# Four slots of a fused attention and gated-MLP kernel get a hand-written order of work on every engine

## The chip, the cores and the metric

The kernel runs on one core of one Trainium2 chip. A core has five engines that run side by side, each from its own queue: TensorE (PE in the profile; the loading of its weights is PEld), VectorE (DVE), ScalarE (ACT), GpSimd (POOL) and SyncE (SP), whose queue issues nearly all DMAs. The metric is the device time of one execution in microseconds, the median of several runs. Before the change it is 759.58 us (three runs, 759.41 to 760.52).

## The reference

```python
def _attn_ref(q, k, v):                      # 8 batches, 8 heads, 576 rows, 64 columns
    scores = scale * np.matmul(q, k.transpose(0, 1, 3, 2))
    scores = np.where(mask, scores, -1e9)    # causal in blocks of 64
    scores = scores - np.max(scores, axis=-1, keepdims=True)
    attn = np.exp(scores)
    attn = attn / (np.sum(attn, axis=-1, keepdims=True) + 1e-09)
    return np.matmul(attn, v)

def _moe_ref(x, w_in, g_ln, w_sg, b_sg, w_out):   # x: 8 x 576 x 512, all heads side by side
    h = gelu_tanh(x @ w_in)                  # 1024 columns
    u, v = h[..., :512], h[..., 512:]
    v_n = (v - mu) / np.sqrt(var + 1e-06) * g_ln  # LayerNorm over columns
    v_s = einsum('ts,bsd->btd', w_sg, v_n) + b_sg[None, :, None]
    return x + (u * v_s) @ w_out
```

The weights w_in, w_out and others arrive as float64 words; results are float32.

## The kernel before

**Accuracy by splits.** TensorE multiplies in float32r, which keeps fewer bits than float32. So every operand x is held as two tiles, hi (x cast to float32r) and lo (x − hi), and each product is made of three: hi·hi, lo·hi, hi·lo. The splits are work for the other engines: q and k on POOL (`split_qk`, line 116, four instructions per slot), the weights on POOL (`split_weight`, line 190, a cast and a subtraction), the attention output x (xh on VectorE, xl on POOL).

**Slots.** The outer loop (line 840) runs over 32 pairs of heads, four to a batch; one round of it is a slot. In slot n TensorE turns (transposes) the probabilities of pair n: pA, pB, pC, then pd and pe, which hold the diagonal blocks and the inverse row sums; the copies ptA, ptB, ptC and rb bring them from PSUM to SBUF (`turn`, `turn_sums`). It makes the scores s of pair n + 1 in two halves (`first` and `second`, each two steps), and between the halves the values product ob of pair n. VectorE takes the maxima and writes prob and negm from the scores, ScalarE makes the exponentials and their sums, VectorE normalises ob to x, and x is written to DRAM (spill) and split.

**FF pieces in the holes.** The MLP of a batch (`feed_forward`, line 542) is cut into pieces that stand in a queue, `work`, and `hole(k)` issues the next k of them between the parts of attention: five v pieces (accv), eight u pieces (accu), eight s pieces (accs, the spatial product) and eight o pieces (acco). A digit string such as "1112" gives the pieces of a slot's four holes. Side steps hang beside them in the queue `side` (line 517): the gelu of v, then five `moments` (bn_stats and bn_aggr), `inverse_std` (rs, on POOL), five `centre` and five `scale` steps (vh on ScalarE, vl on VectorE, the last tile's vn_t and vone on VectorE). `run_side(k)` runs the next k. An s piece needs all of them, and the split spatial weights ws_h and ws_l.

**Weights.** They are loaded and split once, during the first eight slots and a little after. A part is 128 x 256 float64 values. Its sign, exponent and mantissa words are put together to float32 by ScalarE (the Abs of the high word), and three VectorE instructions on words (one shift, two merges), tiles w; POOL then splits it. `load_weight` and `load_spatial` are generators, and each `next` issues one step. v's columns come first, then u's, then the spatial weights (four tiles ws_h/ws_l of 128 rows, then the ends, with the bias b_sg in a zero-filled tile), then w_out.

**Who sets the order.** Slots 0 to 3 (`opening_slot`) hold no FF pieces; there every engine runs in the order in which the program is written (`written`, lines 50 and 145). From slot 4 on only TensorE does (line 842); for the others the framework's scheduler picks the order with a timeline of its own, and weights are issued by `load_share` at places that the table WS gives. PSUM has eight banks (`bank`, line 81), each held from its first product to its last reader. SBUF pages come from small pools: five buffers "pt", shared by the copies ptA to ptC, two buffers "xr" for spatial weights, w_out parts and reloaded spills, two "x", and one each for q_f, k_f and their splits.

Every helper goes through one method (line 60), so the profile gives L60 for almost all instructions and the tiles' names tell them apart.

Of the kernel before, what the change touches and what calls it, by code (L numbers as in the profile page):

```python
# [20 lines left out]
def kernel(  # L21
# [169 lines left out]
        gpsimd.tensor_copy(dh, x)  # L191
        gpsimd.tensor_tensor(dl, x, dh.bitcast(F32), op=ALU.subtract)

    class Double:


        def __init__(self, raw, name):
            n = raw.shape[-1]
            words = raw.bitcast(U32).rearrange("p (n t) -> p n t", t=2)
            self.hi, self.lo = words[:, :, 1], words[:, :, 0]  # L200
            tm = page(U32, 2 * n, name)
            self.t, self.m = tm[:, :n], tm[:, n:]
            scalar.activation(
                self.m.bitcast(F32), self.hi.bitcast(F32), AF.Abs, scale=2.0**-112
            )

        def single(self, words=None):
            t = self.t
            x = t if words is None else words
            vector.tensor_scalar(x, self.lo, 29, None, op0=ALU.logical_shift_right)  # L210
            vector.scalar_tensor_tensor(
                x, self.hi, 0x80000000, x, op0=ALU.bitwise_and, op1=ALU.bitwise_or
            )
            vector.scalar_tensor_tensor(
                t, self.m, 3, x, op0=ALU.logical_shift_left, op1=ALU.bitwise_or
            )
            return t.bitcast(F32)

    def load_weight(part, src, cols, dh, dl, name="w", ahead=2, groups=()):

        W = 256
        parts = [(c, slice(f, f + W)) for f in range(cols.start, cols.stop, W) for c in range(NC)]
        raws = {}

        def fetch(k):
            if k < len(parts):
                c, fs = parts[k]
                raws[k] = page(src.dtype, W, name)
                sync.dma_start(raws[k], src[c * P : (c + 1) * P, fs])

        for k in range(ahead):
            fetch(k)
        if part == "v":
            yield False
        k = 0
        for size in (*groups, *([1] * len(parts))):
            if k == len(parts):
                return
            opened = []
            for j in range(k, k + size):  # L240
                fetch(j + ahead)
                raw = raws.pop(j)
                opened.append(raw if src.dtype == F32 else Double(raw, name))
            yield False
            if src.dtype != F32:
                words = []
                for j, x in enumerate(opened):
                    if part == "v" and j % 2 == 0:
                        t = bank("w").bitcast(U32)
                        words += [t[:, :W], t[:, W:]]  # L250
                opened = [x.single(*words[j : j + 1]) for j, x in enumerate(opened)]
            yield False
            for j, x in zip(range(k, k + size), opened):
                c, fs = parts[j]
                split_weight(x, dh[:, c, fs], dl[:, c, fs])
            k += size
            yield True

    def load_spatial():
        t = page(F32, S, "x")  # L260
        gpsimd.memset(t[BLK:, :DH], 1.0)
        vector.tensor_copy(vone[BLK:, :], t[BLK:, :DH])

        def fetch(j):
            t = page(F32, S, "xr")
            if j < NT - 1:
                sync.dma_start(t, w_sgT[j * P : (j + 1) * P, :])
            elif j == NT - 1:
                for hf in (0, 1):
                    sync.dma_start(t[hf * BLK : (hf + 1) * BLK, :], w_sgT[j * P : S, :])  # L270
            else:
                gpsimd.memset(t[BLK:, :], 0.0)
                sync.dma_start(t[BLK : BLK + 1, :], b_sg.unsqueeze(0))
                sync.dma_start(t[96:97, :], b_sg.unsqueeze(0))
            return t

        raws = deque(fetch(j) for j in (0, 1))
        sync.dma_start(g_bc, g_ln.unsqueeze(0).broadcast_to([P, DH]))
        yield True
        for j in range(NT - 1):  # L280
            split_weight(raws.popleft(), ws_h[:, j, :], ws_l[:, j, :])
            raws.append(fetch(j + 2))
            yield True

        j = NT - 1
        t, t2 = raws
# [8 lines left out]
        yield True  # L295

    weights = deque(
        [
            ("v", load_weight("v", w_in, slice(DH, DFF), wi_h, wi_l, "w", 3, (3, 2, 2, 1))),
            ("u", load_weight("u", w_in, slice(0, DH), wi_h, wi_l)),  # L300
            ("s", load_spatial()),
            ("o", load_weight("o", w_out, slice(0, DM), wo_h, wo_l, "xr", 0)),
        ]
    )

    def weight_half():

# [121 lines left out]
    class Values:  # L429
# [21 lines left out]

# [253 lines left out]
    def hole(k=1):  # L705
# [17 lines left out]

# [16 lines left out]
    def opening_slot(n, va):  # L740
# [37 lines left out]

    def slot(n, va):
        nx = n + 1 < N  # L780
        k = 6 if n // Q == 1 else 3
        g = [int(x) for x in (FIRST if n // Q == 1 else PLAN)[n % Q]]
        if n + 1 < N:
            load_v(n + 1)
# [22 lines left out]
        if nx:  # L807
            nx.second()
        load_share(n, 2)
        if n == Q + 1:  # L810
            run_side(2 * NT + 1)
        if n % Q == Q - 1:
            va.split()
        else:
# [80 lines left out]
```

## Time and profile before

| | |
|---|---|
| median of the runs | 759.58 us |
| the profiled execution | 758.6 us |
| its span, first to last instruction | 756.8 us |
| TensorE busy | 735.5 us, 97% of the span |
| VectorE, ScalarE, GpSimd busy | 467.4, 427.4, 302.2 us |
| mean granted TensorE clock | 0.995 |

The profiled execution is one run, recorded by the hardware. Its span is 1.8 us shorter than its time. Rows of groups show busy time, mean ns of one instruction, and the idle time ahead of it with what ended it; `A <- B` in the waits says that A waited for B. In a timeline a row is start, duration, engine, operation and tiles, and in brackets the idle time ahead. Matmul ends are modelled, so a busy TensorE may still be held back a little.

### The profile page before, as it was taken

What the parts mean: (1) busy time and instruction counts of PE and PEld (TensorE: products, weight loads), DVE (VectorE), ACT (ScalarE), POOL (GpSimd) and SP (SyncE); (2) the same over time, 40 slices, a digit from 0 to 9 for tenths busy, and PEclk for the clock granted to TensorE, in tenths of its full rate; (3) what the DMA queues carried; (4) which work ended last, traced back from release to release, by engine and by line L of the source; (5) the groups of instructions that cost most, each with busy time, mean ns of one, the idle gap of its engine ahead of it and who ended that gap; (6) DMA issues with size and microseconds to landing.
All of it is one profiled execution on the core that took longest, in us unless ns stands there. A gap on an engine that the chain in (4) does not pass through costs nothing.

```text
span 756.8 us, 18453 instructions
## 1 busy us (share of the span) xinstructions
PE 735.5 (97%) x6942; PEld 691.2 (91%) x6942; DVE 467.4 (62%) x1473; ACT 427.4 (56%) x1068; POOL 302.2 (40%) x376
## 2 busy tenths in 40 slices
PE   8999878999999999999999999999999999999997
PEld 6887877989899899999999899998999989998997
DVE  5985869765855369544776348663495545941732
ACT  6894947457644678337764377544873467721500
POOL 3864865644445323243433234351234532322121
PEclk9999999999999999999999999999999999999999
DMA  6545432333342223322233122621234221220032
GB/s 177 169 129 173 127 102 72 98 95 97 110 151 71 65 77 95 106 67 71 71 118 118 33 70 78 187 56 49 66 91 148 71 60 51 61 83 16 6 122 94
DMA packets 84301, 70.05 MB, mean 93 GB/s; under 512 B 59891, under 2 KB 59891, under 8 KB 84213
## 3 DMA queue, kind: packets, MB, share of 16 engines
q1 hardware_dynamic: 84068, 68.58, 30.9%
q8 instruction: 55, 0.90, 0.5%
q10 hardware_dynamic: 144, 0.29, 0.1%
q14 instruction: 34, 0.27, 0.1%
HBM read 49.98 MB, written 18.87 MB: 91 GB/s over the span
## 4 chain that ended last, share of the span: by engine, by line
PE 80%; DVE 6%; ACT 5%; DMA 3%; POOL 2%; issue 2%; DVEq 0%; SPq 0%; ACTq 0%
PE accs L60 15%; PE acco L60 13%; PE accv L60 12%; PE accu L60 11%; PE s L60 10%; PE ob L60 9%; ACT prob L60 3%; PE pd L60 3%; PE pA L60 3%; PE pB L60 3%; DVE prob L60 2%; DMA xr<-in_w_out 2%; PE pC L60 2%; PE pe L60 1%; DVE w L60 1%
## 5 line engine op out<-in xcount | busy, mean ns | idle before, releaser
L60 ACT ACTIVATE prob<-prob,negm 128x576 f32<-128x576 f32 (+3 forms) x320 | 176.6, 555 | 68.0 <-DVE negm L60 66.9
L60 DVE CUSTOM_DVE_ANT_0 prob<-s,mask 128x256 f32<-128x256 f32 (+3 forms) x320 | 119.6, 418 | 42.8 <-PE s L60 41.4
L60 POOL TENSOR_TENSOR xh<-x,xh 128x64 fp32r<-128x64 f32 x32 | 10.5, 328 | 193.2 <-DVE xh L60 171.4
L60 POOL TENSOR_TENSOR gl<-u,gh 128x288 fp32r<-128x288 f32 x64 | 52.2, 820 | 87.1 <-DVE gh L60 71.6
L60 PE MATMUL accu<-xh,wi_h 128*128 128x288 f32 x256 | 78.7, 307 | 3.1 <-DVE negm L60 3.1
L60 PE MATMUL acco<-gh,wo_h 128*128 128x288 f32 x256 | 77.5, 303 | 1.7 <-ACT ptB L60 1.4
L60 PE MATMUL accs<-ws_h,vh 128*128 128x288 f32 x256 | 77.9, 304 | 0.0
L60 PE MATMUL accu<-xh,wi_l 128*128 128x288 f32 x256 | 76.0, 297 | 0.0
L60 PE MATMUL accu<-xl,wi_h 128*128 128x288 f32 x256 | 76.0, 297 | 0.0
L60 PE MATMUL accs<-ws_h,vl 128*128 128x288 f32 x256 | 75.5, 295 | 0.0
L60 PE MATMUL accs<-ws_l,vh 128*128 128x288 f32 x256 | 75.4, 295 | 0.0
L60 PE MATMUL acco<-gh,wo_l 128*128 128x288 f32 x256 | 75.4, 295 | 0.0
L60 PE MATMUL acco<-gl,wo_h 128*128 128x288 f32 x256 | 75.4, 294 | 0.0
L60 PE MATMUL accv<-wi_h,xh 128*128 128x512 f32 x160 | 65.3, 408 | 1.1 <-DVE negm L60 1.1
L60 PE MATMUL s<-kh,qh 64*128 64x320 f32 (+4 forms) x384 | 64.4, 323 | 2.0 <-ACT kh L60 1.3
L60 DVE TENSOR_TENSOR u<-accs,u 128x288 f32<-128x288 f32 x64 | 29.3, 457 | 56.6 <-PE accs L60 55.6
L60 PE MATMUL s<-kh,ql 64*128 64x320 f32 (+4 forms) x384 | 60.0, 303 | 3.9 <-POOL ql L60 3.9
L60 PE MATMUL accv<-wi_l,xh 128*128 128x512 f32 x160 | 62.8, 392 | 0.0
L60 ACT ACTIVATION_READ_ACCUMULATOR prob<-prob,negm 128x1 f32 x320 | 60.3, 189 | 0.0
L60 PE MATMUL s<-kl,qh 64*128 64x320 f32 (+4 forms) x384 | 58.8, 302 | 0.3 <-DVE kl L60 0.3
L60 ACT COPY vv<-accv 128x512 f32<-128x512 f32 x32 | 18.6, 581 | 64.8 <-PE accv L60 64.8
L60 PEld LDWEIGHTS accu<-xh,wi_h 128*128 128x128 f32 x256 | 48.5, 189 | 4.7 <-issue 3.0
(116 smaller groups left out, 2081.1 us busy)
## 6 DMA issues: line engine op xcount, KB each, us to landing
q_f<-in_qT SPq DMA_DIRECT2D x32, 288.0 KB, 3.4
spill<-x SPq DMA_DIRECT2D x32, 288.0 KB, 2.8
xr<-spill SPq DMA_DIRECT2D x32, 288.0 KB, 3.0
out_T<-xr SPq DMA_DIRECT2D x32, 288.0 KB, 3.1
k_f<-in_kT SPq DMA_DIRECT2D x31, 288.0 KB, 3.3
v_f<-in_v SPq DMA_DIRECT2D x32, 128.0 KB, 2.9
v_d<-in_v SPq DMA_DIRECT2D x64, 64.0 KB, 2.6
v_f<-in_v SPq DMA_DIRECT2D x64, 64.0 KB, 2.6
```

What stands on the lines that cost most here:

```text
L60: return lambda *a, **k: pin(method(*a, **k), self.letter)
```

## The change

The float64 weights are handled in pairs of parts (size 2): two Abs, two shifts and two merges of 256 columns into a PSUM bank, one merge of 512 columns, and one cast and one subtraction of 2 x 256 on POOL in place of two each. w_out keeps single parts, now in the "pt" buffers. The DMAs of all weights stand in one list, `coming`, and `fetch(k)` issues the next k where the script says. Slots 4 to 7 become `middle_slot`, and every engine runs them in the order written; six entries of SCRIPT a slot say what is issued between the parts of attention. Slots from 8 on stay with the scheduler. In slots 4 to 7 the ptC copy goes to ScalarE. On TensorE nothing moves: its rows are the same, but for 10 filler transposes in place of 16 ahead of slot 0.

```diff
-    class Double:
-            scalar.activation(
-                self.m.bitcast(F32), self.hi.bitcast(F32), AF.Abs, scale=2.0**-112
-            )
...
+    def fetch(k=1):
+
+        for _ in range(k):
+            coming.popleft()()
...
+    def load_weight(src, off, cols, dh, dl, name, size):
...
+            raw = [raws.popleft() for _ in range(size)]
...
+            if size == 2:
+                m = page(U32, size * W, name)
+            else:
+                tm = sp.tile([P, 2 * W], U32, tag="pt", name="tm", bufs=5)
+                t, m = tm[:, :W], tm[:, W:]
+            for j, x in enumerate(words):
+                scalar.activation(
+                    m[:, j * W : (j + 1) * W].bitcast(F32),
+                    x[:, :, 1].bitcast(F32),
+                    AF.Abs,
+                    scale=2.0**-112,
+                )
+            yield False
+            if size == 2:
+                t = page(U32, size * W, name)
+                y = bank("w").bitcast(U32)
+            else:
+                y = t
+            for j, x in enumerate(words):
+                yj = y[:, j * W : (j + 1) * W]
+                vector.tensor_scalar(yj, x[:, :, 0], 29, None, op0=ALU.logical_shift_right)
+                vector.scalar_tensor_tensor(
+                    yj, x[:, :, 1], 0x80000000, yj, op0=ALU.bitwise_and, op1=ALU.bitwise_or
+                )
+            vector.scalar_tensor_tensor(
+                t, m, 3, y, op0=ALU.logical_shift_left, op1=ALU.bitwise_or
             )
...
+            split_weight(t, *dst)
             yield True
...
+    def fetch_ends():
+        t = page(F32, S, "xr")
+        for hf in (0, 1):
+            sync.dma_start(t[hf * BLK : (hf + 1) * BLK, :], w_sgT[(NT - 1) * P : S, :])
+        t2 = page(F32, S, "xr")
+        gpsimd.memset(t2[BLK:, :], 0.0)
+        sync.dma_start(t2[BLK : BLK + 1, :], b_sg.unsqueeze(0))
+        sync.dma_start(t2[96:97, :], b_sg.unsqueeze(0))
+        raws.extend((t, t2))
...
-            copy("a" if which == "C" and self.n < Q else TE[which], pt, t)
+            copy("a" if which == "C" and self.n < 2 * Q else TE[which], pt, t)
...
-    WS = {
-        4: (0, 4, 0, 2),
...
+    WS = {8: (0, 0, 1, 3), 9: (0, 0, 0, 2)}
...
+        fetch(2 if n < Q - 1 else 4)
...
+    def weigh(k=1):
+        for _ in range(k):
+            weight_half()
+
+    SCRIPT = {
+        4: (
+            lambda: (fetch(2), weigh(1)),
+            lambda: weigh(3),
+            lambda: (fetch(2), weigh(3)),
+            lambda: None,
+            lambda: weigh(3),
+            lambda: (fetch(3), weigh(2)),
+        ),
+        5: (
+            lambda: (run_gelu(), weigh(1), fetch(1)),
+            lambda: run_side(2),
+            lambda: (run_side(3), weigh(1), fetch(1)),
+            lambda: run_side(1),
+            lambda: weigh(1),
+            lambda: None,
+        ),
+        6: (
+            lambda: (run_side(5), weigh(1), fetch(1)),
+            lambda: (run_side(4), weigh(1)),
+            lambda: run_side(1),
+            lambda: None,
+            lambda: fetch(1),
+            split_pending,
+        ),
+        7: (
+            lambda: None,
+            lambda: None,
+            lambda: None,
+            lambda: weigh(2),
+            lambda: weigh(1),
+            lambda: weigh(3),
+        ),
+    }
+
+    def middle_slot(n, va):
...
+        va.turn("A0")
+        va.turn("A1")
+        if n != 2 * Q - 2:
+            split_pending()
+        hole(g[0])
+        script[0]()
+        va.turn("B0")
+        va.turn("B1")
+        hole(g[1])
+        script[1]()
+        va.turn("C")
+        va.turn_sums()
+        hole(g[2])
+        script[2]()
+        nx = Scores(n + 1)
+        nx.first()
+        va.products()
+        va.normalise()
+        nx.second()
...
+        nv.inverse()
+        script[3]()
+        split_qk(n + 2)
+        script[4]()
+        hole(g[3])
+        script[5]()
+        return nx, nv
...
-    warm(bank("warm"), 16)
+    warm(bank("warm"), 10)
...
-        if n == Q:
+        if n == 2 * Q:
             written.intersection_update("P")
-        sc, va = (opening_slot if n < Q else slot)(n, va)
+        sc, va = (opening_slot, middle_slot, slot)[min(n // Q, 2)](n, va)
```

What moves is best seen on three engines. First VectorE in the first half of slot 4, before (ISA with prob and negm is the maximum step on the scores s, and w are the words of u's columns):

```order
L60 COPY ptA_1076<-pA_1075 128x512
L60 TENSOR_SCALAR r<-sums 128x10
L60 RECIPROCAL r<-r 128x10
L60 COPY ptB_1105<-pB_1104 128x512
L60 COPY ptC<-pC 128x512
L60 TENSOR_SCALAR w<-w 128x256
L60 SCALAR_TENSOR_TENSOR w<-w 128x256
L60 TENSOR_SCALAR w<-w 128x256
L60 SCALAR_TENSOR_TENSOR w<-w 128x256 x2
L60 TENSOR_SCALAR w<-w 128x256
L60 ISA prob_110,negm<-s,mask 128x256
L60 ISA negm 128x1
```

and after:

```order
L60 COPY ptA_1065<-pA_1064 128x512
L60 COPY ptB_1101<-pB_1100 128x512
L60 TENSOR_SCALAR w<-w 128x256
L60 SCALAR_TENSOR_TENSOR w<-w 128x256
L60 TENSOR_SCALAR w<-w 128x256
L60 SCALAR_TENSOR_TENSOR w<-w 128x256
L60 SCALAR_TENSOR_TENSOR w<-w 128x512
L60 TENSOR_SCALAR w<-w 128x256
L60 SCALAR_TENSOR_TENSOR w<-w 128x256
L60 TENSOR_SCALAR w<-w 128x256
L60 SCALAR_TENSOR_TENSOR w<-w 128x256
L60 SCALAR_TENSOR_TENSOR w<-w 128x512
```

The words of one part, and the last steps of others among the maxima, have become the words of two groups of two parts, all ahead of the first maximum.

Second, POOL around slot 6, before (ws_h and ws_l are the split spatial weights, rs LayerNorm's inverse deviation, sums and xr fills, qh to kl the splits of the pair after next):

```order
L60 TENSOR_TENSOR ws_l<-xr,ws_h 128x576 x2
L60 CAST kh<-k_f 128x576
L60 CAST qh<-q_f 128x576
L60 MEMSET sums 128x2
L60 CAST ws_h<-xr 128x576 x2
L60 TENSOR_TENSOR kl<-k_f,kh 128x576
L60 TENSOR_SCALAR rs<-stats 128x5
L60 TENSOR_TENSOR ql<-q_f,qh 128x576
L60 TENSOR_TENSOR ws_l<-xr,ws_h 128x576 x2
L60 TENSOR_TENSOR rs<-rs,half 128x5
L60 MEMSET xr 64x576
L60 CAST ws_h<-xr 128x576
```

and after:

```order
L60 TENSOR_SCALAR rs<-stats 128x5
L60 TENSOR_TENSOR rs<-rs,half 128x5
L60 CAST qh<-q_f 128x576
L60 TENSOR_TENSOR ql<-q_f,qh 128x576
L60 CAST kh<-k_f 128x576
L60 TENSOR_TENSOR kl<-k_f,kh 128x576
L60 CAST ws_h<-xr 128x576
L60 TENSOR_TENSOR ws_l<-xr,ws_h 128x576
L60 CAST ws_h<-xr 128x576
L60 TENSOR_TENSOR ws_l<-xr,ws_h 128x576
L60 MEMSET xr 64x576
L60 CAST ws_h<-xr 128x576
```

The four steps of q and k stood among the spatial weights and rs; now rs, then q and k whole, then each spatial tile with its cast and subtraction together.

Third, ScalarE in slot 6, before (u copies a u piece from PSUM, vh is LayerNorm's scale step, the cast ws_l the row of the bias):

```order
L60 COPY ptB_1745<-pB_1744 128x512
L60 COPY u<-accu 128x288
L60 COPY rb<-pd 128x512
L60 COPY rb<-pe 128x384
L60 COPY u<-accu 128x288
L60 ACTIVATE prob_107,sums<-prob_107,negm 128x192 x2
L60 ACTIVATE vh<-vv,rs 128x512 x3
L60 CAST ws_l<-xr 64x576
```

and after:

```order
L60 COPY ptB_1694<-pB_1693 128x512
L60 COPY u<-accu 128x288
L60 ACTIVATE vh<-vv,rs 128x512 x3
L60 CAST ws_l<-xr 64x576
L60 COPY ptC<-pC 128x512
L60 COPY rb<-pd 128x512
L60 COPY rb<-pe 128x384
L60 COPY u<-accu 128x288
L60 ACTIVATE vh<-vv,rs 128x512
```

The scale steps and the bias cast stood behind the rb copies, among the exponentials; now three of them and the bias cast stand ahead of ptC and rb.

More of the change, by code (lines that the diff above doesn't have):

```diff
@@ L192, in split_weight @@
         gpsimd.tensor_tensor(dl, x, dh.bitcast(F32), op=ALU.subtract)
-    class Double:
[L197 to L202, printed above, removed]
-            scalar.activation(
-                self.m.bitcast(F32), self.hi.bitcast(F32), AF.Abs, scale=2.0**-112
-            )
[L207 to L212, printed above, removed]
-            )
[L214 to L233, printed above, removed]
-            yield False
[L235 to L256, printed above, removed]
@@ new lines, with fetch_weight, fetches @@
+    W = 256
+    raws = deque()
+    coming = deque()
+    def fetch(k=1):
+        for _ in range(k):
+            coming.popleft()()
+    def fetch_weight(src, c, fs, name):
+        t = page(src.dtype, W, name)
+        sync.dma_start(t, src[c * P : (c + 1) * P, fs])
+        raws.append(t)
+    def fetches(src, cols, name):
+        for f in range(cols.start, cols.stop, W):
+            for c in range(NC):
+                coming.append(lambda c=c, f=f: fetch_weight(src, c, slice(f, f + W), name))
@@ L262, in load_spatial @@
         vector.tensor_copy(vone[BLK:, :], t[BLK:, :DH])
[L264 to L279, printed above, removed]
         for j in range(NT - 1):
             split_weight(raws.popleft(), ws_h[:, j, :], ws_l[:, j, :])
-            raws.append(fetch(j + 2))
             yield True
         j = NT - 1
-        t, t2 = raws
+        t, t2 = raws.popleft(), raws.popleft()
         gpsimd.tensor_copy(ws_h[:, j, :], t)
@@ L295, in load_spatial, with fetch_spatial, fetch_gain @@
         yield True
+    def fetch_spatial(j):
+        t = page(F32, S, "xr")
+        sync.dma_start(t, w_sgT[j * P : (j + 1) * P, :])
+        raws.append(t)
+    def fetch_ends():
+        t = page(F32, S, "xr")
+        for hf in (0, 1):
[5 more added lines that the diff above has]
+        raws.extend((t, t2))
+    def fetch_gain():
+        sync.dma_start(g_bc, g_ln.unsqueeze(0).broadcast_to([P, DH]))
     weights = deque(
         [
-            ("v", load_weight("v", w_in, slice(DH, DFF), wi_h, wi_l, "w", 3, (3, 2, 2, 1))),
-            ("u", load_weight("u", w_in, slice(0, DH), wi_h, wi_l)),
+            ("v", load_weight(w_in, DH, DH, wi_h, wi_l, "w", 2)),
+            ("u", load_weight(w_in, 0, DH, wi_h, wi_l, "w", 2)),
             ("s", load_spatial()),
-            ("o", load_weight("o", w_out, slice(0, DM), wo_h, wo_l, "xr", 0)),
+            ("o", load_weight(w_out, 0, DM, wo_h, wo_l, "xr", 1)),
         ]
     )
+    fetches(w_in, slice(DH, DFF), "w")
+    fetches(w_in, slice(0, DH), "w")
+    coming.append(fetch_gain)
+    for j in range(NT - 1):
+        coming.append(lambda j=j: fetch_spatial(j))
+    coming.append(fetch_ends)
+    fetches(w_out, slice(0, DM), "xr")
     def weight_half():
@@ L780, in slot @@
         nx = n + 1 < N
-        k = 6 if n // Q == 1 else 3
+        k = 3
         g = [int(x) for x in (FIRST if n // Q == 1 else PLAN)[n % Q]]
@@ L826, in slot @@
         return nx, nv
+    def weigh(k=1):
[36 more added lines that the diff above has]
+    def middle_slot(n, va):
+        script = SCRIPT[n]
+        g = [int(x) for x in FIRST[n % Q]]
+        load_v(n + 1)
+        load_qk(n + 2)
+        va.turn("A0")
[17 more added lines that the diff above has]
+        nx.second()
+        if n % Q == Q - 1:
+            va.split()
+        else:
+            pending.append(va.split)
+        nv = Values(n + 1, nx)
+        nv.inverse()
[5 more added lines that the diff above has]
+        return nx, nv
     pending = []
@@ L832 @@
     load_qk(1)
-    next(weights[0][1])
+    fetch(2)
     sc = Scores(0)
```

28 lines of the change are left out of this document (21 added, 7 removed).

## The prediction

> **What bounds the kernel now.** I read the page's first part, then a table of windows cut at the first pA transpose of each slot (slot n treats head pair n; slot 4 starts at 53.0 us), then TensorE's waits, then the timelines where TensorE stood still.
>
> ```profile
> span 756.8 us, 18453 instructions
> PE 735.5 (97%) x6942; PEld 691.2 (91%) x6942; DVE 467.4 (62%) x1473; ACT 427.4 (56%) x1068; POOL 302.2 (40%) x376
> ...
> 53.00:76.80 23.80, 22.62 (x184) 19.14 (x183) 14.92 (x52) 12.85 (x36) 11.76 (x17) 1.00 0.55 159
> 76.80:95.10 18.30, 16.00 (x175) 15.01 (x174) 15.54 (x48) 17.22 (x44) 15.69 (x21) 1.00 0.42 129
> 95.10:120.30 25.20, 18.52 (x176) 17.74 (x175) 19.22 (x43) 11.94 (x31) 15.79 (x14) 0.89 0.29 79
> 120.30:145.90 25.60, 24.94 (x239) 23.85 (x238) 22.32 (x64) 17.22 (x43) 15.90 (x20) 0.98 0.31 92
> 145.90:168.00 22.10, 22.10 (x184) 18.99 (x183) 13.52 (x44) 10.23 (x28) 10.08 (x15) 1.00 0.34 101
> 168.00:191.20 23.20, 22.38 (x224) 21.53 (x223) 12.72 (x46) 18.71 (x48) 11.41 (x17) 1.00 0.34 98
> 191.20:215.00 23.80, 22.26 (x225) 21.46 (x224) 21.12 (x61) 16.96 (x39) 10.85 (x11) 1.00 0.37 116
> ...
> 239.10:261.10 22.00, 22.00 (x183) 18.95 (x182) 8.98 (x34) 10.88 (x29) 6.35 (x9) 1.00 0.20 55
> 261.10:283.10 22.00, 22.00 (x224) 21.48 (x223) 11.52 (x40) 16.63 (x41) 6.48 (x9) 1.00 0.29 78
> 283.10:305.00 21.90, 21.90 (x224) 21.39 (x223) 18.91 (x55) 16.50 (x36) 9.19 (x10) 1.00 0.36 113
> 305.00:329.10 24.10, 24.10 (x240) 23.59 (x239) 14.11 (x47) 8.70 (x25) 10.16 (x14) 1.00 0.33 95
> ```
>
> The columns are the stretch, its length, busy time of PE, PEld, DVE, ACT and POOL, the granted clock, and the DMA share. TensorE is busy for 735.5 of 756.8 us: it is the bound. The last four rows are slots 12 to 15, with TensorE never idle at full clock; they show what a slot costs when nothing makes it wait. Slot 12 holds five v pieces (22.0), slot 13 eight u pieces (22.0), slot 14 eight o pieces (21.9), slot 15 eight s pieces (24.1). Slots 4, 8, 9, 10 and 7 hold the same TensorE work as 12, 12, 13, 14 and 15. Slots 5 and 6 hold four u pieces; one piece is
>
> ```profile
> 86.17 1.59 PE accu L60 x12
> ...
> 89.34 2.80 PE ob L60 x56
> ...
> 92.26 1.25 PE s L60 x12
> ```
>
> (chain of waits) 1.59 us, so their floor is 22.0 − 4 × 1.59 = 15.6. What each slot loses against its floor: slot 4, 23.8 − 22.0 = 1.8; slot 5, 18.3 − 15.6 = 2.7; slot 6, 25.2 − 15.6 = 9.6; slot 7, 25.6 − 24.1 = 1.5; slot 8, 0.1; slot 9, 23.2 − 22.0 = 1.2; slot 10, 23.8 − 21.9 = 1.9. Together 18.8 us. The order on TensorE is the same row for row before and after, but for six filler transposes; so the change can only give back waits, and these 18.8 us are nearly all there is.
>
> ```profile
> PE s L60 <- POOL ql L60: 3.9, 1, 3.9
> PE accu L60 <- DVE negm L60: 3.1, 2, 2.8
> PE accv L60 <- DVE negm L60: 1.1, 1, 1.1
> ...
> 103.28 0.38 PE L60 MATMUL s<-kh,qh 64*128 64x256 f32 x2
> 107.53 0.43 PE L60 MATMUL s<-kh,ql 64*128 64x256 f32 x2 [3.86 <-POOL ql L60]
> ```
>
> Slot 6 is the large one: TensorE's score products stand 3.9 us for the split of q on POOL, then 2.8 us for VectorE. The clock falls after each: 0.89 of 25.2 us and 0.98 of 25.6 us leave out 2.8 + 0.5 = 3.3 us, 1.65 us for each of the two waits.
>
> **The change, slot by slot.** All times below are from the slot's first pA.
>
> Opening slots: VectorE's word work goes from 3, 2, 2, 1 weight parts to 2 each, the same eight parts. Slot 0 is relieved of one part, slot 3 gets one more. By
>
> ```profile
> L60 DVE SCALAR_TENSOR_TENSOR w<-w 128x256 uint32<-128x256 uint32 x32 | 14.5, 466 | 1.3
> L60 DVE TENSOR_SCALAR w<-w 128x256 uint32<-128x256 uint32 x16 | 7.8, 499 | 4.7 <-DMA w<-in_w_in 4.6
> ```
>
> a part is 0.50 + 2 × 0.47 = 1.4 us, so the bounds are −1.0 and +0.9; I take 0. The six filler transposes fewer ahead of slot 0 lie under ScalarE's first exponentials:
>
> ```profile
> 10.09 4.01 ACT prob L60 x15
> ...
> 56.91 0.87 PE pB L60 x8
> ```
>
> that chain of waits runs through them, not through the fillers: 0, and at most 6 × 0.87 / 8 = 0.65 if it did not.
>
> Slot 4. The words of the first u columns were fetched here and came late:
>
> ```profile
> 64.75 0.39 PE L60 MATMUL s<-kh,qh 64*128 64x256 f32 x2
> ...
> 65.20 0.29 DVE L60 TENSOR_SCALAR w<-w 128x256 uint32<-128x256 uint32 x1 [3.50 <-DMA w<-in_w_in]
> ...
> 68.51 0.41 DVE L60 CUSTOM_DVE_ANT_0 prob<-s,mask 128x256 f32<-128x256 f32 x1
> ```
>
> VectorE stood 3.5 us for the DMA, then did words while the scores, begun at 64.75, waited until 68.51; their banks came free late and the next v piece stood 1.1 us. Afterwards the first four parts are fetched in slot 3, and two groups of two parts stand ahead of the scores on VectorE: four shifts, four 256-wide merges and two 512-wide ones (between 0.47 and 0.94, I take 0.7) are 5.3 us, from the ptB copy at about 5.4 to 10.7, while scores come at 64.75 − 53.0 = 11.7. They fit with 1 us over. Left: 0.4 (0 to 1.8), for the extra part in slot 3.
>
> Slot 5. After the reciprocal (1.5 before the slot) VectorE does two more groups (5.3) and the vv add, then ptA, the xh cast and the 1.0-fill copy to vone, then ptB, and five
>
> ```profile
> L580 DVE BATCH_NORM_STATS2 bs<-vv 128x6 f32<-128x512 f32 x8 | 5.3, 661 | 0.0
> ```
>
> with their aggregates, some 4 us, ahead of the softmax of the scores. I reach 11 us there; the scores are ready at 8.7. A new wait stands in that row: vone reads a tile that POOL fills only behind the last w split and xl. TensorE has ob (2.8) to do meanwhile and six banks in use, so only the second half of the next scores and one u piece feel it. Left: 0.8 (0 to 2.7).
>
> Slot 6, the term that decides. POOL's queue is now: q and k split for slot 7, ws rows 2 and 3, a fill, ws row 4.
>
> ```profile
> L60 POOL TENSOR_TENSOR ws_l<-xr,ws_h 128x576 fp32r<-128x576 f32 x4 | 5.6, 1414 | 0.0
> L60 POOL TENSOR_TENSOR ql<-q_f,qh 128x576 fp32r<-128x576 f32 x13 | 18.6, 1428 | 0.5
> L60 POOL CAST qh<-q_f 128x576 fp32r<-128x576 f32 x13 | 8.8, 676 | 12.4 <-PE s L60 5.9 <-DVE negm L60 5.3 <-DMA q_f<-in_qT 1.2
> L60 POOL MEMSET xr<- 64x576 f32 x1 | 0.6, 573 | 0.1
> ...
> 99.99 3.25 POOL L60 CAST ws_h<-xr 128x576 fp32r<-128x576 f32 x1 [3.26 <-DMA xr<-in_w_sgT]
> ...
> 100.01 3.77 DVE L586 SCALAR_TENSOR_TENSOR vv<-vv,stats,g_bc 128x512 f32<-128x512 f32 x5
> ```
>
> The split starts when slot 5's last scores are done: ob from 9.8, 2.80 and 1.25 make 13.9 of 15.6, so 1.7 before the slot. It takes 2 × (0.68 + 1.43) = 4.2 and ends at 2.5, far ahead of the scores, which ask for it at 103.28 − 95.1 = 8.2: the 3.9 us wait goes. But the five centring steps start at 2 to 4, and the last two rows show what they do to POOL: a cast that takes 0.68 elsewhere took 3.25, to the last of the five. So rows 2 and 3 of ws, 2 × 2.1, finish at 2.5 + 3.7 + 4.2 = 10.4, and the fill at 11.0. Behind the fill stands the DMA of b_sg (a small DMA lands after 2.0), behind that, on ScalarE's queue, the cast of ws_l, and behind it ptC and both rb copies, without which ob cannot run:
>
> ```profile
> L60 ACT COPY ptC<-pC 128x512 f32<-128x512 f32 x4 | 2.3, 581 | 0.0
> L60 ACT COPY rb<-pd 128x512 f32<-128x512 f32 x12 | 7.0, 585 | 6.6 <-PE pd L60 6.4
> L60 ACT COPY rb<-pe 128x384 f32<-128x384 f32 x12 | 5.8, 486 | 0.0
> L60 ACT CAST ws_l<-xr 64x576 fp32r<-64x576 f32 x1 | 0.7, 669 | 0.0
> ...
> v_d<-in_v SPq DMA_DIRECT2D x64, 16.0 KB, 2.0
> ```
>
> 13.0 + 0.67 + 0.58 + 0.59 + 0.49 = 15.3. TensorE is ready for ob at 8.2 + 1.6 = 9.8, so it stands 5.5 us, and its clock falls once, 1.65. The second wait of before, on the banks, is covered by this one. Left: 7.1 (2.3 to 9.6).
>
> The page "SBUF — State Buffer" of the Trainium skill (section "Who interferes with whom") says that a VectorE instruction with two SBUF inputs and a GpSimd instruction that reads SBUF exclude each other, and that whichever issues first has the shared port pair for that whole instruction. The trace agrees that they exclude each other, and not on the length: the cast waited through a run of five, 3.25 us. By the page alone POOL would get its turn after each step, which is rival (a).
>
> Slot 7: LayerNorm and spatial weights are done before it, the half clock at its start is gone, and its eight s pieces wait for the gelu of u only. Left 0.3 (0 to 1.5). Slots 8 to 10 keep the scheduler; the w_out words move later (six parts in slots 8 and 9 where five stood in slot 8) and ScalarE no longer puts vh ahead of ptB in slot 10. Left 0.1, 0.6 and 0.6 of 0.1, 1.2 and 1.9 (0 to 3.5 together).
>
> Sum: 0.4 + 0.8 + 7.1 + 0.3 + 0.1 + 0.6 + 0.6 = 9.9 us lost, where 18.8 were: −8.9. The profiled execution took 758.6 (span 756.8 and 1.8 around it), which becomes 749.7; it lies 1.0 under the median of the runs, 759.58, so I predict 750.7.
>
> **The rivals.** (a) POOL gets its turn after each centring step. Row 2 is done at 2.5 + 2.1 = 4.6; then a step of 3.77 / 5 = 0.75, the cast 0.68, a step, the subtraction 1.41: 8.2, the fill at 8.8, b_sg at 10.8, rb at 13.1. Ob is 3.3 late and the clock falls once: slot 6 loses 5.0, and the time is 748.6. For it: no row shows a run of five beside a POOL queue that is already moving; against it: the 3.25 row. 0.2. The page named above would give this case. (b) POOL's chain slips ahead, since the exponentials end late and centring starts after row 3: fill at 2.5 + 4.2 + 0.6 = 7.3, ob at 11.6, slot 6 loses 2 to 3, the other slots nothing or little: 742 to 747, say 745. The rows leave POOL barely 2 us for it. 0.13. (c) Slot 6 gains nothing, because VectorE's later two-input steps (vn_t, vl) hold POOL a second time: another 3 us on 7.1 is 10.1. Then only slots 4, 5, 7, 9 and 10 give: −8.9 + 3 = −5.9, or −4 where 9 and 10 keep theirs: 754.5. 0.14.
>
> (d) Slower. The w_out words move from xr tiles into the five buffers of the pt copies. In slots 8 and 9 a ptB or ptC copy then waits until POOL has split a part, and POOL's queue puts that behind q and k: 4.2, and 3.25 if centring holds the port, 7.5 a slot, 15 in two; less the 8.9 saved, +6: 766. It decides when those copies come over 4.5 us after TensorE is ready for ob in both slots; my own sum for slot 9 has them 2 us early. 0.06. (e) No change, savings and new waits balancing: 0.06.
>
> **How the numbers follow.** Forecast 0.41, rivals as above. The time is the forecast's, 750.7. Low end: (b) down to 743. High end: (c) with slot 3's extra 0.9 and slots 9 and 10 unchanged, 756.5. Left out are (d), (e) and the tip of (b). About 0.2% (1.5 us) is what a measurement here tells from no change. Faster: 0.41 + 0.2 + 0.13 + 0.14 = 0.88; same 0.06; slower 0.06.
>
> **What would show it.** Right: in the table of windows slot 5 at 16 to 17 us and slot 6 at 21 to 24 with one clock dip; in slot 6 the pieces up to the first scores run unbroken, then ob waits for an rb copy, ScalarE's ws_l cast waits for a DMA of b_sg, and POOL's ws_h cast is long beside the centring. Wrong: a slot 6 under 19 us; a wait of s for ql still there; a slot 5 over 18; pt copies that wait for wo_l in slots 8 and 9.

## The result, and the profile after

The changed kernel takes 749.52 us (median of 4 runs, 748.33 to 749.84) where the kernel before takes 759.79 beside it (759.41 to 760.52): a ratio of 0.9861, with an interval of 0.9844 to 0.9878. Forecast were 750.7, between 743.0 and 756.5. The profiled execution after took 748.33, with a span of 746.5, against 758.6 and 756.8: 10.3 less in both.

The table of windows after, cut as before at the first pA of slots 4 to 10 (columns as in the prediction):

```profile
51.80:74.90 23.10, 22.49 (x185) 19.01 (x184) 17.75 (x57) 16.61 (x50) 15.60 (x17) 1.00 0.64 192
74.90:92.50 17.60, 16.29 (x176) 15.20 (x175) 13.68 (x43) 12.72 (x29) 13.38 (x16) 1.00 0.39 103
92.50:114.80 22.30, 18.16 (x177) 17.34 (x176) 20.53 (x51) 15.03 (x43) 12.01 (x13) 0.85 0.32 88
114.80:138.80 24.00, 24.00 (x239) 23.49 (x238) 17.45 (x48) 16.88 (x41) 14.70 (x21) 1.00 0.36 96
138.80:160.90 22.10, 22.10 (x185) 19.00 (x183) 15.73 (x48) 11.02 (x31) 9.90 (x15) 1.00 0.29 84
160.90:182.90 22.00, 22.00 (x224) 21.52 (x223) 17.46 (x49) 18.47 (x45) 12.12 (x17) 1.00 0.44 130
182.90:205.10 22.20, 21.96 (x224) 21.41 (x223) 20.63 (x59) 16.61 (x36) 9.70 (x13) 1.00 0.36 111
```

Against the floors of the prediction:

| slot | 4 | 5 | 6 | 7 | 8 | 9 | 10 | sum |
|---|---|---|---|---|---|---|---|---|
| lost before | 1.8 | 2.7 | 9.6 | 1.5 | 0.1 | 1.2 | 1.9 | 18.8 |
| forecast | 0.4 | 0.8 | 7.1 | 0.3 | 0.1 | 0.6 | 0.6 | 9.9 |
| lost after | 1.1 | 2.0 | 6.7 | 0 | 0.1 | 0 | 0.3 | 10.2 |

The seven slots give 8.7 (162.0 to 153.3), the stretch ahead of them, now 51.8 long instead of 53.0, gives 1.2, and 0.4 lie behind them. TensorE's waits in slots 0 to 10 after:

```profile
PE ob L60 <- ACT ptC L60: 3.1, 1, 3.1
...
PE s L60 <- DVE negm L60: 1.2, 2, 0.9
PE s L60 <- DVE ptB L60: 1.1, 1, 1.1
PE accv L60 <- POOL xl L60: 0.6, 1, 0.6
```

The 3.9 us wait of s for ql and the 2.8 us one for VectorE are gone. A wait of ob for ScalarE stands there instead, where the forecast put it. But the timelines of slot 6 show another chain than the forecast's. ScalarE:

```profile
98.61 1.37 ACT L60 ACTIVATE vh<-vv,rs 128x512 fp32r<-128x512 f32 x2
104.77 0.72 ACT L60 ACTIVATE vh<-vv,rs 128x512 fp32r<-128x512 f32 x1 [4.78 <-DVE vn_t L60]
105.51 0.67 ACT L60 CAST ws_l<-xr 64x576 fp32r<-64x576 f32 x1
106.20 0.59 ACT L60 COPY ptC<-pC 128x512 f32<-128x512 f32 x1
```

ScalarE stands 4.8 us for VectorE's vn_t step, not for the DMA of b_sg: its ws_l cast runs without a wait. VectorE and POOL at that time:

```profile
90.94 0.67 POOL L60 CAST qh<-q_f 128x576 fp32r<-128x576 f32 x1 [0.49 <-PE s L60]
...
95.93 1.43 POOL L60 TENSOR_TENSOR ws_l<-xr,ws_h 128x576 fp32r<-128x576 f32 x1
97.31 1.12 POOL L60 CAST ws_h<-xr 128x576 fp32r<-128x576 f32 x1
98.51 1.76 POOL L60 TENSOR_TENSOR ws_l<-xr,ws_h 128x576 fp32r<-128x576 f32 x1
100.33 0.57 POOL L60 MEMSET xr<- 64x576 f32 x1
```

```profile
96.58 5.55 DVE L604 SCALAR_TENSOR_TENSOR vv<-vv,stats,g_bc 128x512 f32<-128x512 f32 x5
102.07 0.67 DVE L60 COPY ptB<-pB 128x512 f32<-128x512 f32 x1
102.67 0.47 DVE L60 TENSOR_SCALAR vone<-vv,rs 64x512 fp32r<-64x512 f32 x1
103.17 0.42 DVE L60 CAST vn_t<-vone 64x512 fp32r<-64x512 f32 x1
103.60 1.13 DVE L60 SCALAR_TENSOR_TENSOR vn_t<-vv,rs,vone 64x512 fp32r<-64x512 f32 x1
```

The five centring steps take 5.55 us instead of 3.77; POOL's cast takes 1.12, not 3.25. The two engines take turns, as in rival (a): the first centring step begins at 96.58, POOL's cast at 97.31, the second step at 97.83, POOL's subtraction at 98.51 and the third step at 98.90, each while the one before it still runs.

```profile
97.83 1.15 DVE L604 SCALAR_TENSOR_TENSOR vv<-vv,stats,g_bc 128x512 f32<-128x512 f32 x1
98.90 1.92 DVE L604 SCALAR_TENSOR_TENSOR vv<-vv,stats,g_bc 128x512 f32<-128x512 f32 x1
```

VectorE pays more than POOL: the five steps are 1.8 us longer than before, the cast and the subtraction together 0.8 (1.12 and 1.76 for 0.67 and 1.43).

### The profile page after: what moved, and what is told of

Same layout as the page of the kernel before. It is cut to its first block, busy times and chain, and to the rows that moved or that the text cites. A ratio compares the mean times of both kernels' runs of the same rounds, so it can differ in the third digit from the quotient of the medians.

```text
span 746.5 us, 18406 instructions
## 1 busy us (share of the span) xinstructions
PE 732.5 (98%) x6936; PEld 689.4 (92%) x6936; DVE 469.3 (63%) x1461; ACT 429.2 (57%) x1072; POOL 295.2 (40%) x360
## 4 chain that ended last, share of the span: by engine, by line
PE 84%; DVE 7%; ACT 5%; issue 2%; DMA 1%; POOL 0%; ACTq 0%; DVEq 0%; POOLq 0%
PE accs L60 16%; PE acco L60 13%; PE accv L60 12%; PE accu L60 11%; PE s L60 10%; PE ob L60 10%; ACT prob L60 4%; PE pA L60 3%; PE pB L60 3%; PE pd L60 3%; PE pC L60 2%; DVE prob L60 2%; PE pe L60 1%; DVE vv L604 1%; DVE bs L598 1%
## 5 line engine op out<-in xcount | busy, mean ns | idle before, releaser
L60 POOL CAST kh<-k_f 128x576 fp32r<-128x576 f32 x31 | 20.9, 674 | 75.7 <-PE s L60 75.7
```

Source lines behind the costliest of these rows:

```text
L60: return lambda *a, **k: pin(method(*a, **k), self.letter)
```

## The experiments

The theory formed from that trace: ob waits because VectorE's LayerNorm steps in slot 6 are late. They start late (slot 5's loss), they are stretched by POOL's splits on the port, and they reach ScalarE through a page: the nine pages of vv, vh and vl are all taken at the third vh, and vn_t's step gives the first one back. The rival is the forecast's chain: POOL's late fill, the b_sg DMA, the ws_l cast. The profiled executions are compared slot by slot, since even one opening code starts slot 1 at 21.4 in one execution and at 22.8 in another.

**1. The bias rows behind rb.** Slot 6's script:

```diff
-            lambda: (run_side(4), weigh(1)),
-            lambda: run_side(1),
+            lambda: run_side(4),
+            lambda: (weigh(1), run_side(1)),
```

> The changed kernel with the last spatial row (its bias rows, ScalarE's ws_l cast among them) moved in slot 6 from ahead of the pC transposes to behind the rb copies; nothing else. Forecast's theory (ScalarE stands for the DMA of b_sg, and ptC and rb stand behind its ws_l cast): ob starts when TensorE is ready, the 3.1 us wait of ob goes, slot 6 shrinks from 22.3 to about 19, the time is 744 to 746. Rival, read from the trace after (ScalarE stands for vn_t, because the third vh needs the page of vv that vn_t frees): only the 0.67 of the cast itself comes off the wait, ob still waits 2.4, slot 6 is 21.6, the time 748 to 749.5.

```profile
106.38 0.72 ACT L60 ACTIVATE vh<-vv,rs 128x512 fp32r<-128x512 f32 x1 [5.78 <-DVE vn_t L60]
```

Measured 749.43 (748.83 to 750.63), slot 6 22.8, and ob waits 3.3. The forecast's chain falls: the cast no longer stands ahead of ptC, and ob waits all the same, for vn_t. Against the changed kernel's profile not even the cast's own 0.67 is won, since POOL's last split fell on the vn_t step, which took 1.79 instead of 1.13. That is not the edit's doing: run 4, whose slot 6 has the changed kernel's orders, shows the same (below), and ob waits 4.1 there. Against that run the wait is 0.8 shorter, about what the rival expects.

```profile
104.01 1.79 DVE L60 SCALAR_TENSOR_TENSOR vn_t<-vv,rs,vone 64x512 fp32r<-64x512 f32 x1
```

**2. The scale steps behind rb as well.**

```diff
-            lambda: (run_side(4), weigh(1)),
-            lambda: run_side(1),
+            lambda: None,
+            lambda: (run_side(4), weigh(1), run_side(1)),
```

> The changed kernel with both the scale steps of LayerNorm (vn_t, three vh and vl) and the last spatial row moved in slot 6 behind the rb copies. ScalarE then has nothing that waits ahead of ptC and rb. Both theories: ob does not wait for ptC. Theory of the page of vv: all of the 3.1 us wait is gone here and was not without the scale steps' move. What comes next: VectorE's order is unchanged, so the second scores wait for banks until its softmax, behind the vl steps, is done: a new wait of s for negm of 2 to 3 us; slot 6 loses 4 to 5.5 instead of 6.7; the time is 746 to 748. If VectorE were not the next limit, slot 6 would lose 1.1 (the ptB wait) and the time would be 743.

TensorE's one long wait in slots 6 and 7:

```profile
111.78 1.22 PE L60 MATMUL s<-kh,qh 64*128 64x320 f32 x2 [4.33 <-DVE negm L60]
```

Measured 749.76 (749.66 to 751.06), slots 6 and 7 22.6 and 25.0. Ob no longer waits for ScalarE, and the second scores wait 4.3 us for VectorE, more than I expected. So ScalarE's order was only the place where the lateness showed; VectorE is the bound in slot 6.

**3. vone filled in the opening.** `load_spatial` loses its fill and copy, and ahead of slot 0 stand

```diff
+    ones = page(F32, S, "x")
+    gpsimd.memset(ones[BLK:, :DH], 1.0)
...
+    vector.tensor_copy(vone[BLK:, :], ones[BLK:, :DH])
```

> The changed kernel with the fill of ones and its copy to vone done once in the opening, ahead of slot 0, instead of in slot 5 behind POOL's last w split and xl. Theory (VectorE's 3.4 us stand for that fill is what makes slot 5 lose 2.0 and hands its lateness to slot 6): five bn end 3 us earlier, slot 5 loses 0 to 0.5, and in slot 6 the reciprocal, the centring and vn_t start 1 to 2 us earlier against the slot's start, so ob waits 1.5 to 2 instead of 3.1; the time is 744 to 746, and down to 742 if the half clock does not come. Rival (the stand is hidden, since the bn and ptB steps would hold VectorE anyway): slot 5 loses 1.5 or more, the time is 748 to 749.5.

The wait that it takes out of slot 5, in the changed kernel's VectorE timeline:

```profile
83.59 0.42 DVE L60 CAST vone<-x 64x512 fp32r<-64x512 f32 x1 [3.41 <-POOL x L60]
```

Slots 5 and 6 in the windows of this run, and its centring:

```profile
76.40:92.00 15.60, 15.60 (x175) 15.05 (x174) 14.77 (x47) 14.35 (x35) 12.52 (x15) 1.00 0.53 138
92.00:114.60 22.60, 18.15 (x177) 17.34 (x176) 19.98 (x43) 13.51 (x37) 12.56 (x13) 0.85 0.26 75
```

```profile
94.16 6.98 DVE L600 SCALAR_TENSOR_TENSOR vv<-vv,stats,g_bc 128x512 f32<-128x512 f32 x5
```

Slot 5 is at its floor, TensorE never idle, so all its 2.0 came from that stand. Slot 6 gained nothing: the centring starts earlier, but then all five steps lie beside POOL and take 7.0, and ob waits 3.9. The time is 748.65 (747.53 to 749.17), not the 744 to 746 of the theory.

**4. Six more fillers.** `warm(bank("warm"), 16)` again.

> The changed kernel with sixteen filler transposes ahead of slot 0 again instead of ten. Forecast (they lie under ScalarE's first exponentials): the first pA is 0.65 later and the wait of pA for prob goes for it, slot 1 starts within 0.2 of the changed kernel's, the time stays at 749.5 within 0.5. Rival (they are on the path): all starts move by 0.65, the time is 750.2.

749.45 (748.85 to 750.59). The first pA comes at 10.92 instead of 10.29; pA's second half waited 0.43 for prob in the changed kernel and does not here; slot 1 starts at 21.4 in both. The fillers cost nothing.

**5. The port left to VectorE.** Row 4 is treated like rows 2 and 3:

```diff
-            split_weight(raws.popleft(), ws_h[:, j, :], ws_l[:, j, :])
+            x = raws.popleft()
+            if j < 2:
+                split_weight(x, ws_h[:, j, :], ws_l[:, j, :])
...
+    for j in (2, 3, 4):
+        gpsimd.tensor_copy(ws_h[:, j, :], z)
+        gpsimd.tensor_copy(ws_l[:, j, :], z)
```

> The changed kernel with POOL's splits of spatial rows 2, 3 and 4 left out (those parts of the spatial weights are zeros, filled in the opening), so that POOL has nothing to do in slot 6 from the end of the q and k split; VectorE's and ScalarE's orders are the same. Theory (each two-input VectorE step stands for POOL's turn on the port): the five centring steps take 3.7 to 3.8 instead of 5.55, vn_t 0.74 instead of 1.13, so vn_t ends 2.2 earlier, the 1.05 wait for ptB goes, ob waits 1 to 2 instead of 3.1, slot 6 is 20.1 with the same half clock, 17 to 18.5 with less of it; the time 745.5 to 747.5. Rival (the forecast's: a run of five keeps the port and only POOL stands): the centring is as long as before, 5.5, and slot 6 changes by no more than what the bias rows' fill gives, under 0.7.

```profile
98.84 3.38 DVE L602 SCALAR_TENSOR_TENSOR vv<-vv,stats,g_bc 128x512 f32<-128x512 f32 x5
...
103.69 0.74 DVE L60 SCALAR_TENSOR_TENSOR vn_t<-vv,rs,vone 64x512 fp32r<-64x512 f32 x1
```

```profile
94.70:112.90 18.20, 16.12 (x177) 15.27 (x176) 15.51 (x46) 13.46 (x37) 4.86 (x7) 1.00 0.31 90
```

The centring, begun 4.1 us after the slot's start as in the changed kernel, takes 3.4 us and vn_t 0.74; ob waits 2.0 instead of 3.1, the ptB wait is gone, the clock stays at 1.00, and slot 6 is 18.2: 4.1 shorter, with TensorE's, VectorE's and ScalarE's orders unchanged. The two waits of slot 6 fall from 3.09 + 1.05 to 2.0, by 2.1; most of the other 2.0 is the half clock that did not come, and that is not settled by this edit. Measured 747.00 (746.63 to 747.99): the profiled execution is the fastest, and in two of the other three the mean clock is 0.995 and 0.992. The one at 0.995, the clock of all four runs of the changed kernel, took 747.29, 2.2 under their median. So POOL's splits beside VectorE make about half of what TensorE waits in slot 6.

**6. The last tile's scale step behind the first three.**

```diff
-        for st in (NT - 1, *range(NT - 1)):
+        for st in (0, 1, 2, NT - 1, 3) if b == 0 else (NT - 1, *range(NT - 1)):
```

> The changed kernel with the first batch's scale steps in another order: vh and vl of tiles 0, 1 and 2 first, the last tile's vone and vn_t behind them, tile 3 as before. The same instructions in the same places of the program otherwise. Theory of the page (ScalarE's third vh stands until a page of the vv tiles is given back, by whichever step reads one first): the first vl, at 102.7 on the clock of the changed kernel's trace, frees one at 103.4, so the third vh starts 1.3 earlier, and ws_l, ptC, rb and ob with it, unless the b_sg DMA, issued at 101.3, then holds ws_l: ob waits 1.6 to 2.2 instead of 3.1, slot 6 is 1 to 1.5 shorter (up to 4.5 where the half clock goes too); the time 745 to 748.5. Theory of the forecast (the b_sg DMA behind ws_l): no change in the wait, 749.5. Rival (vh needs what the last tile's step computes): the wait grows to 5 or more.

```profile
106.30 0.72 ACT L60 ACTIVATE vh<-vv,rs 128x512 fp32r<-128x512 f32 x1 [3.44 <-DVE vl L60]
107.05 0.67 ACT L60 CAST ws_l<-xr 64x576 fp32r<-64x576 f32 x1
```

```profile
95.40:116.00 20.60, 17.80 (x176) 16.93 (x174) 18.56 (x46) 13.38 (x37) 12.07 (x13) 0.92 0.28 80
```

The third vh is now released by the first vl. Ob waits 1.8 and slot 6 is 20.6, with one stretch of half clock instead of two; the time, 748.34 (746.71 to 749.60), is not clear of the changed kernel's. Slot 5 of the profiled execution lost 1.5 more, after a stand for weights in slot 4 as in run 10. The rows show that a page is what it waits for: vh needs nothing that vn_t computes, only a tile that is read and free. The ws_l cast still does not wait, so the b_sg DMA is not next either.

**7. Spatial rows earlier.** On top of 3, rows 0 and 1 are split in slot 4, rows 2 and 3 in slot 5.

```diff
-            lambda: (fetch(2), weigh(3)),
+            lambda: (fetch(2), weigh(3), rows(2)),
...
-            lambda: (run_side(3), weigh(1), fetch(1)),
+            lambda: (run_side(3), rows(2), fetch_ends()),
```

> The kernel with vone early, and besides POOL's splits of spatial rows 0 and 1 moved into slot 4 (POOL is idle there) and of rows 2 and 3 into slot 5, so that in slot 6 only the q and k split and the last row's short part are left to POOL. VectorE's and ScalarE's orders are unchanged. Theory (VectorE's LayerNorm steps in slot 6 are stretched because each waits its turn with a POOL instruction on the SBUF port: five centring steps took 7.0 us with vone early, 5.6 in the changed kernel, 3.8 before): the five take 4 to 5.6, vn_t ends 1.5 to 3 earlier, ob waits 1 to 2.5 instead of 3.9, slot 6 falls from 22.6 to 19.5 to 21, the time is 745 to 747. Rival (the centring is long for another reason, its own waits): the five take 6 or more, slot 6 stays over 22, the time at 748.6.

749.66 (748.01 to 751.44): slot 6 falls to 20.2 with ob waiting 2.7, as the theory has it, though the centring still takes 5.5, beside the k split and the last row. But slot 5 grows to 19.5, so nothing is left of it. What happened shows in run 9.

**8. The same with the order of 2,** the scale steps and the last row behind rb.

> The one above, and ScalarE's ptC and rb copies ahead of the scale steps, as in the run with scale and bias late. Theory (VectorE's total work ahead of its softmax is the bound in slot 6, so this order only pays when that work has become shorter): ob does not wait, the second scores wait 1 to 2.5 us for negm instead of 4.3, slot 6 is 18 to 19.5, the time 744 to 746. Rival (the order of ScalarE was the bound): the wait for negm is gone too, slot 6 is 16.5, the time 742.5. If the order does not matter: as the run above.

748.45 (748.07 to 749.29): slot 6 20.0, slot 7 25.1, with 2.9 us of waiting for negm, above what I expected, and slot 6 and the time miss the 18 to 19.5 and 744 to 746 of the theory. Ob does not wait, but the runs overlap with those of run 7, so what the order is worth stays open.

**9. Two centring steps ahead of the reciprocal,** and slot 6's second ptB copy on ScalarE.

```diff
+        if n == 5:
+            run_side(3)
         nv = Values(n + 1, nx)
```

> The one above, and two of the five centring steps ahead of the reciprocal at the end of slot 5, where VectorE stands 1.3 us for the last exponentials, and slot 6's second ptB copy on ScalarE instead of VectorE (0.67). Theory (VectorE bounds slot 6): 1.3 to 2 us less ahead of its softmax; slot 6 is 16.5 to 18, the time 742.5 to 744.5. Rival (the reciprocal, 1 to 2 us later by this, holds rx and so the pd transposes): pd waits up to 1 us and half of that is lost.

746.30 (744.34 to 746.72): slots 6 and 7 are 19.8 and 24.2, and no pd waits. Slot 6 and the time miss the theory's 16.5 to 18 and 742.5 to 744.5. What 7 to 9 have in common is on ScalarE in slot 4; here it is in 9 (3.06 and 3.36 in 7 and 8):

```profile
73.11 0.35 ACT L60 ACTIVATE prob<-prob,negm 64x64 f32<-64x64 f32 x1 [3.56 <-POOL sums L60]
```

The exponentials need a small fill of sums, which stood behind the moved rows on POOL: the mistake that slot 5 paid for.

**10. The rows behind that fill.**

```diff
-            lambda: (fetch(2), weigh(3), rows(2)),
-            lambda: None,
+            lambda: (fetch(2), weigh(3)),
+            lambda: rows(2),
```

> The run with centring ahead, with POOL's spatial rows moved behind the fill of the softmax sums: in slot 4 rows 0 and 1 from ahead of the second scores to behind them, in slot 5 rows 2 and 3 likewise (ahead of the rs steps). In the run with centring ahead ScalarE stood 3.6 us in slot 4 for that fill, the exponentials ended 3 late, and slot 5 lost 1.4 (pB waits for a bank behind vt). Theory (that stand costs slot 5 its 1.4 and hands 1.5 us of lateness on VectorE to slot 6, which then waits 2.1 for negm and falls to half clock): slot 5 is 15.6 to 16, slot 6 16.5 to 18 instead of 19.8, the time 741.5 to 744. Rival (slot 6 is set by its own 8 us of POOL beside VectorE, however early it starts): slot 5 as above, slot 6 over 19, the time 744.5 to 745.5.

744.16 (742.28 to 746.66), a ratio to the kernel before of 0.9802 (0.978 to 0.9823). In the profiled execution, the slowest of the five, slot 5 is 15.9 and slot 6 20.1. That alone would speak for the rival, and the median lies between the two ranges; but here ScalarE stood 2.4 us in slot 4 for the DMA of the last u words, and slot 6 may have inherited it.

**11. Those u words fetched first.**

```diff
+        if n == 4:
+            fetch(4)
         load_v(n + 1)
```

> The run above, with the last four u parts fetched at the head of slot 4's DMA queue, ahead of v, q and k of the next pair, instead of behind them. In the traces so far ScalarE stood between 0 and 2.0 us in slot 4 for these parts, another amount in each execution, ahead of the exponentials. Theory (these parts land just in time): that stand is gone, the time is 0 to 1 under the run above, and its runs lie closer together. Rival (v, q and k for the next pair come later by it and something waits for them): 0.5 or more above.

```profile
76.10:91.70 15.60, 15.60 (x176) 15.09 (x175) 14.79 (x48) 14.36 (x35) 14.45 (x18) 1.00 0.33 96
91.70:108.90 17.20, 16.17 (x176) 15.15 (x175) 16.91 (x37) 12.05 (x32) 7.52 (x8) 1.00 0.27 74
```

743.03 (741.25 to 743.77), a ratio of 0.9785 (0.9768 to 0.9802): 6.5 us under the changed kernel, and the best here. ScalarE does not stand for words in slot 4 (nor did it in run 5, without this move), slot 6 loses 1.6, and the clock does not fall. Its lead over run 10 is not settled, since the intervals overlap; its runs do lie closer together, 2.5 us wide against 4.4.

**12. w_out where it was,** three parts in slot 7 and five in slot 8.

```diff
-    WS = {8: (0, 0, 1, 3), 9: (0, 0, 0, 2)}
+    WS = {8: (0, 2, 0, 3)}
```

> The changed kernel with the parts of w_out where they stood before: three in slot 7 and five in slot 8 (two ahead of the B transposes, three at its end), none in slot 9; their words still in the pt buffers. Slots 9 and 10 lost 1.2 and 1.9 us before and lose 0 and 0.3 in the changed kernel. Theory (the parts in slot 8 made that loss): slots 9 and 10 lose 2 to 3 again, the time is 751.5 to 752.5. Rival (the scheduler's other order there, gelu's table load ahead of the ptA copy, follows from timing elsewhere): no loss, 749.5. Rival of the pt buffers: with five parts in slot 8 the pt copies wait, slot 8 or 9 loses over 3, 753 or more.

751.07 (750.30 to 751.27), but not from there: slots 8, 9 and 10 are 22.1, 21.9 and 22.0, without loss. In the profiled execution the time lies in slot 5 (20.0 instead of 17.6), after a 2.0 us stand for the u words. Whether it does in the other three is not shown, and the ratio's interval, 0.9869 to 0.9907, overlaps the changed kernel's. So the place of the w_out parts does not decide about slots 9 and 10. Their words stayed in the pt buffers here, so what leaving the xr tiles is worth was not tried.

## Why the prediction was right, and where it was not

**The sum.** 9.9 us were to be left in slots 4 to 10, 10.2 are; the opening was put at 0 and gave 1.2. The time is 1.2 under the forecast. The errors of the slots, worked out below, are +0.7, +1.2, −0.4 and −1.2 (slots 7 to 10): that they cancel to 0.3 is luck.

**Slot 4: 0.4, measured 1.1.** The words of the two groups take 5.1 us (5.3 worked out) and are in time, though they begin 7.4 after the slot's start and not 5.4. Of what is lost, 0.6 is accv waiting for xl behind slot 3's extra group on POOL. What I missed is that the second four parts come just in time: ScalarE stood from 0 to 2.4 us ahead of them, another amount in each execution (in four of these the profile names a VectorE step as the releaser of part of it). That lateness seems to reach slots 5 and 6 (runs 10 to 12).

**Slot 5: 0.8, measured 2.0.** The mechanism was named, the size was off: the stand for the fill, 3.4 us, was hidden in a sum that reached 11 us after the slot's start, while the first maximum came at 13.9 (the row below, against 74.9). Run 3 shows it to be the whole loss. At 17.6 the slot lies between the sign of being right (16 to 17) and the sign of being wrong (over 18).

```profile
88.76 0.38 DVE L60 CUSTOM_DVE_ANT_0 prob<-s,mask 128x256 f32<-128x256 f32 x1
```

**Slot 6: 7.1, measured 6.7: the right size by a wrong chain.** Right: q and k start 1.6 ahead of the slot (1.7 forecast), the wait for ql goes, ob waits for ScalarE, the clock falls. Wrong is the step "a cast that takes 0.68 elsewhere took 3.25, to the last of the five", from which the fill, the DMA and the ws_l cast were reckoned. One row had been made a rule. POOL's fill ended at 8.4 after the slot's start, forecast 11.0 and rival (a) 8.8. Rival (a)'s turn-taking was the true mechanism, but its way from POOL's fill to ob was the forecast's and falls with it, and it too left out that VectorE pays: 5.55 − 3.38 = 2.2 us on the centring alone. The page of the vv tiles was not in the forecast at all. Ob started 14.3 after the slot's start, forecast 15.3: VectorE's lateness happened to be about as long as the chain that I had built.

```profile
106.84 0.47 PE L60 MATMUL ob<-ptA,v_f 128*64 128x128 f32 x1 [3.09 <-ACT ptC L60]
```

Nor did ob wait for an rb copy. It begins 0.05 after the ptC copy ends, with both rb copies, 1.08 of the 15.3, still to end. By the count of the eight banks (four s, pC, pd, pe and the last accu) it needed the one that the ptC copy frees; no run tests that. TensorE was ready for ob at 11.3, not 9.8, since the scores had waited 1.05 for the second ptB copy, behind the long centring on VectorE. So the forecast's 7.1 is 5.5 of waiting and 1.65 of clock, and the 6.7 is 4.1 of waiting in two places, about 2.1 of clock and some 0.4 of rest.

The page "SBUF — State Buffer" of the Trainium skill (section "Who interferes with whom") says that the one who issues first holds the port for that whole instruction and the other one is blocked. The trace after agrees: the first centring step (the row below), begun at 96.58 beside a subtraction that ran to 97.36, took 1.32 us, against 3.38 / 5 = 0.68 in run 5 with nothing beside it. The cast of 3.25 before stays unexplained and goes against that page of the Trainium skill, since it began 0.02 us ahead of the first centring step and yet was the one that waited. No other execution here has one like it.

```profile
96.58 1.32 DVE L604 SCALAR_TENSOR_TENSOR vv<-vv,stats,g_bc 128x512 f32<-128x512 f32 x1
```

**The clock: once 1.65, measured 3.35.** 0.15 of 22.3 us: one fall, as forecast, but twice as long as either before. About 1.2 of it lay on the wait itself; what fell on work is 0.27 of the 7.96 us behind the wait, 2.1, so the sum hardly felt it.

```profile
106.84:114.80 7.96, 7.96 (x85) 7.65 (x86) 7.74 (x30) 6.42 (x21) 1.48 (x2) 0.73 0.11 40
```

**Slots 7 to 10: 1.6, measured 0.4.** Slot 10 is free as reckoned. Its loss before began on ScalarE:

```profile
199.53 0.72 ACT L60 ACTIVATE vh<-vv,rs 128x512 fp32r<-128x512 f32 x1 [3.16 <-POOL rs L60]
200.16 0.57 ACT L60 COPY ptB<-pB 128x512 f32<-128x512 f32 x1
```

Afterwards ptB stands ahead of vh. In run 12 vh is ahead again and costs nothing, since rs is there; so the late rs was needed for the loss. Why rs was late before was not tried. Rival (d)'s wait came, which was a sign of being wrong, but it was small: in slot 8 the ptC copy waits 1.31 us for POOL's split of w_out (below), in slot 9 ptA and ptB 0.75 and 0.70, and TensorE stands for none of them.

```profile
147.50 0.69 DVE L60 COPY ptC<-pC 128x512 f32<-128x512 f32 x1 [1.31 <-POOL wo_l L60]
```

**The opening: 0, measured −1.2.** Slot 1 is 10.1 in all runs and was 10.7, which fits VectorE's even groups but was not tried. The other 0.6, ahead of slot 1, is less than executions of one code differ there.

## What to carry to other kernels

When one wait is taken away, work out from when the engine behind it is free, not only what else stands in the queue: here three different orders of slot 6 (the changed kernel's and those of runs 1 and 2) all ended at VectorE, at 22.3 to 22.8 us, and the slot became shorter when POOL's splits went from beside VectorE's steps (runs 5 and 7) or when a page was given back earlier (run 6). A split moved to an idle stretch of GpSimd must be read against everything that stands behind it in that queue, however small: a 0.1 us fill behind the moved splits made ScalarE stand for over 3 us. And one long instruction in a trace is an event, not a rule; look for a second one before building on it.

## What the runs showed of the hardware

A wait of TensorE has no fixed price in clock. By the granted clock of the windows, it was at half speed (0.50 in the first row below, a window inside such a stretch of run 10) for about 3.4 us or about 6.8 us or not at all: not after 2.0 us in run 5, one stretch after waits of 1.0 and 1.8 in run 6 (0.92 of 20.6 us), two after 1.9 in run 10:

```profile
107.00:113.00 6.00, 5.98 (x25) 5.32 (x26) 4.57 (x23) 5.57 (x20) 4.03 (x4) 0.50 0.32 95
91.60:111.70 20.10, 18.17 (x175) 16.89 (x174) 19.43 (x48) 15.19 (x41) 11.12 (x12) 0.88 0.35 101
111.70:136.80 25.10, 25.10 (x240) 24.57 (x239) 15.91 (x48) 16.67 (x40) 13.48 (x19) 0.96 0.32 89
```

0.12 × 20.1 + 0.04 × 25.1 = 3.4 us of speed lost, 6.8 at half. The Trainium skill ("TensorE: Matmul & The Clock Gate", Part 1, "What's actually happening") has a free-running window of 3.413 us that decides; stretches of one or two such windows, whatever the wait, agree with that. The table of that section of the Trainium skill puts the slow clock after at least one idle window; here the one wait of 1.9 us in run 10 was enough, and the measurement decides.
